# Gate and up products of two token blocks made 256 columns at a time

## The chip, the cores and the metric

The kernel runs on one core of a Trainium2 chip, in one launch. The core has a matrix engine (PE, with its weight loads shown apart as PEld), a vector engine (DVE), a scalar engine (ACT), a general engine (POOL) and a queue engine (SP) that issues most of the transfers. On-chip data lie in 128 partitions; matrix products land in PSUM, in tiles of 128 by 512 floats here. The metric is the device time of the whole launch in microseconds; lower is better.

## The reference

The reference is one transformer-like layer for 2048 tokens of width 640: a modulation vector, a layer norm, a long convolution (a state space kernel applied by FFT), a second layer norm, and a gated feed-forward part of width 1728. The change touches only the feed-forward part:

```python
def _B_ref(x, w1, w3, w2):
    gate = jnp.einsum("bsd,df->bsf", x, w1)
    up = jnp.einsum("bsd,df->bsf", x, w3)
    h = _silu(gate) * up
    out = jnp.einsum("bsf,fd->bsd", h, w2)
    return out
...
x = x + ga * _A_ref(h, ...)
h = _layernorm(x, axis=-1) * (1 + cb) + sb
x = x + gb * _B_ref(h, B_w1, B_w3, B_w2)
```

Everything is float32.

## The kernel before

The first 390 us or so make the convolution. The rest is the feed-forward part, in `ffn` (L755). It runs over four token blocks `b` of 512 tokens, and in each over 14 tiles of 128 hidden columns (`ORDER`: tile 0, then tile 13, which is half as wide, then 1 to 12).

To keep float32 accuracy at the rate of the type float32r, each operand is split into a high and a low part (`split`, L665): `x` into `xh` and `xl`, `w1` and `w3` into `wh` and `wl`, the hidden values into `ah` and `al`, `w2` into `w2h` and `w2l`. A product is three terms: high by high, high by low, low by high.

For each tile three steps follow each other in the program:

- `up` (L792) makes the gate and the up product, each in a PSUM tile `gu` of 128 hidden columns by 512 tokens: for each of the five 128-wide slices `k` of the width it makes the three terms `wh·xh`, `wh·xl`, `wl·xh` (L800 to L802), 15 matmuls that add into one tile. Each matmul has weights of 128 by 128 and a moving operand of 128 by 512. Tile 13 holds gate and up in one `gu`. A block so has 27 `gu` tiles and 405 such matmuls.
- `gate` (L805) makes the hidden values from the two tiles: a tanh on ACT (L813), two DVE operations (L814, L815), the split into `ah` and `al` (L666, L667). For tile 13 it is a longer chain over 64 partitions (L819 to L826).
- `down` (L829) multiplies the hidden values of the tile before by `w2` into the five accumulators `acc0` to `acc4` of the block: 15 matmuls a tile, 10 for tile 13.

The weights of each tile are loaded by SP (L713, L718) and split by ACT and DVE (L732, L733, L741, L745) ahead of their use. After the eighth tile of a block, `ln2` (L669) norms and transposes the next block's tokens into `xh` and `xl`; after a block's last tile `output` (L839) adds the result and stores it.

The `gu` tiles have three PSUM banks in turn, `wr`, `wh`, `wl`, `ah`, `al` two buffers each. Within these limits and the data's own order a scheduler of the build sets the order of the instructions on each engine; the engines then run their lists in order and wait for each other by semaphores.

Of the kernel before, what the change touches and what calls it, by code (L numbers as in the profile page):

```python
# [21 lines left out]
KT = D // P  # L22
# [260 lines left out]
class K:  # L283
# [508 lines left out]
    def up(self, b, tiles, xh, xl, ps):  # L792

        nc = self.nc
        gu = [[ps.tile([P, 512], F32, name=f"gu{b}_{m}{i}", tag="gu", bufs=3) for i in range(2 if m < 13 else 1)] for m, _, _ in tiles]
        every = [(pg, wh[:, i], wl[:, i]) for (m, wh, wl), g in zip(tiles, gu) for i, pg in enumerate(g)]
        for ks in [(k,) for k in range(KT)] if len(tiles) > 1 else [range(KT)]:
            for pg, wh, wl in every:
                for k in ks:
                    nc.tensor.matmul(pg, wh[:, k, :], xh[:, k, :], start=(k == 0), stop=False)  # L800
                    nc.tensor.matmul(pg, wh[:, k, :], xl[:, k, :], start=False, stop=False)  # L801
                    nc.tensor.matmul(pg, wl[:, k, :], xh[:, k, :], start=False, stop=(k == KT - 1))  # L802
        return gu

    def gate(self, b, m, gu, pool):  # L805
# [764 lines left out]
```

## Time and profile before

| | |
|---|---|
| time, median of 2 runs | 985.68 us (984.6 to 986.76) |
| the profiled execution's own time | 987.09 us |
| its span, first to last instruction | 985.3 us |
| PE / PEld busy, share of the span | 90% / 72% |
| DVE / ACT / POOL busy, share of the span | 68% / 50% / 29% |
| granted TensorE clock, mean | 0.972 |
| first matmul of the second block's `gu` | 553.79 us into the span |
| first matmul of the third block's `gu` | 694.82 us |
| first matmul of the fourth block's `gu` | 835.85 us |

The profile gives for each instruction its engine, source line, tiles and shape, its start and its length. The length of a matmul is modelled and reaches into the next one, since matmuls are pipelined: how fast a row of matmuls runs is read from their starts, not from their lengths. The start of one to the start of the next is called the step here. The float32r operands of matmuls are shown as f32 in the rows.

### The profile page before, as it was taken

To read this page: it belongs to the slowest core of one execution; us is meant where nothing else is said; L and a number is where in the kernel's file an instruction comes from. 1 tells how busy PE (TensorE), PEld (TensorE's weight loads), DVE (VectorE), ACT (ScalarE), POOL (GpSimd) and SP (SyncE) were. 2 spreads that over 40 slices of the span, in tenths; PEclk is the share of its full clock that TensorE was granted. 3 is DMA by queue.
4 is the path that set the end of the run, shared out by engine and by line. 5 is a ranking of instruction groups with operands and counts; after the bars stand their busy time and mean duration, and the time that the engine had idled before them with its cause. 6 is when DMAs were issued, how large, how long until landed. Compare 5 with 4: busy or idle time off the path is not lost.

```text
span 985.3 us, 20196 instructions
## 1 busy us (share of the span) xinstructions
PE 884.0 (90%) x8095; PEld 707.7 (72%) x8095; DVE 665.6 (68%) x1235; ACT 496.6 (50%) x829; POOL 287.9 (29%) x293
## 2 busy tenths in 40 slices
PE   1465787889999997999999999999999999999997
PEld 1133665767888873677788888888888888888885
DVE  6998999999999774677664464464644554754443
ACT  6878788879888741532243343342333333433321
POOL 0798799889899330100000000000000000000000
PEclk9885999999999999999999999999999999999999
DMA  9955453714131297997232354223353323543311
GB/s 207 271 173 200 115 140 89 176 46 118 36 94 45 62 271 217 223 234 181 58 111 76 107 150 118 80 85 103 100 154 93 108 80 93 141 120 88 104 31 53
DMA packets 141189, 122.03 MB, mean 124 GB/s; under 512 B 13480, under 2 KB 124840, under 8 KB 139688
## 3 DMA queue, kind: packets, MB, share of 16 engines
q1 hardware_dynamic: 140360, 119.84, 45.3%
q8 instruction: 63, 1.03, 0.5%
q10 hardware_dynamic: 736, 0.92, 0.3%
q14 instruction: 30, 0.25, 0.1%
HBM read 99.75 MB, written 20.97 MB: 123 GB/s over the span
## 4 chain that ended last, share of the span: by engine, by line
PE 70%; DVE 15%; ACT 4%; DMA 3%; issue 3%; SPq 2%; POOL 2%; DVEq 0%; ACTq 0%; POOLq 0%
PE acc L837 19%; PE gu L800 12%; PE gu L801 12%; PE gu L802 12%; DVE yy L157 3%; PE ps L157 3%; PE kps L157 2%; SPq L157 2%; DVE fp L157 2%; PE fz L157 2%; DVE hn L157 2%; DVE xx L157 2%; PE fk L157 2%; PE fh L157 2%; PE iy L652 1%
## 5 line engine op out<-in xcount | busy, mean ns | idle before, releaser
L800 PE MATMUL gu<-xh,wh 128*128 128x512 f32 x540 | 210.8, 392 | 0.1
L802 PE MATMUL gu<-xh,wl 128*128 128x512 f32 x540 | 210.3, 390 | 0.0
L801 PE MATMUL gu<-xl,wh 128*128 128x512 f32 x540 | 210.3, 390 | 0.0
L732 ACT ACTIVATE wh<-wr 128x640 fp32r<-128x640 f32 x105 | 71.9, 731 | 134.3 <-PE gu L801 131.0
L744 POOL MEMSET w2l<- 64x640 f32 x3 | 1.9, 630 | 444.6 <-PE acc L837 444.6
L800 PEld LDWEIGHTS gu<-xh,wh 128*128 128x128 f32 x540 | 101.7, 189 | 21.3 <-ACT xh L666 0.5
L802 PEld LDWEIGHTS gu<-xh,wl 128*128 128x128 f32 x540 | 101.4, 188 | 21.2
L801 PEld LDWEIGHTS gu<-xl,wh 128*128 128x128 f32 x540 | 101.6, 188 | 20.8
L813 ACT ACTIVATE th<-gu 128x512 f32<-128x512 f32 x52 | 31.1, 597 | 128.7 <-PE gu L802 128.5
L815 DVE TENSOR_TENSOR a<-a,gu 128x512 f32<-128x512 f32 x52 | 35.8, 688 | 85.6 <-PE gu L802 85.4
L157 POOL TENSOR_TENSOR yy<-e,e 128x512 f32<-128x512 f32 x80 | 86.2, 1093 | 16.5 <-PE kps L157 10.5
L814 DVE SCALAR_TENSOR_TENSOR a<-th,gu 128x512 f32<-128x512 f32 x52 | 35.7, 686 | 75.2 <-ACT th L813 75.1
L837 PE MATMUL acc<-w2h,ah 128*128 128x512 f32 x219 | 85.4, 390 | 0.0
L837 PE MATMUL acc<-w2l,ah 128*128 128x512 f32 x219 | 85.4, 390 | 0.0
L733 ACT ACTIVATE w2h<-w2r 128x640 fp32r<-128x640 f32 x54 | 39.9, 739 | 88.7 <-issue 52.2
L741 DVE TENSOR_TENSOR wl<-wr,wh 128x640 fp32r<-128x640 f32 x105 | 82.4, 819 | 0.0
L157 POOL TENSOR_TENSOR ph<-p,p 128x1024 int32<-128x1024 int32 x40 | 79.9, 1996 | 7.7 <-ACT tr L157 7.0
L745 DVE TENSOR_TENSOR w2l<-w2r,w2h 128x640 fp32r<-128x640 f32 (+1 forms) x54 | 44.4, 822 | 52.9 <-ACT w2h L733 52.7
L157 DVE TENSOR_TENSOR yy<-yy,tr 128x512 f32<-128x512 f32 (+1 forms) x80 | 75.5, 945 | 0.9 <-ACT tr L157 0.6
L837 PE MATMUL acc<-w2h,al 128*128 128x512 f32 x203 | 76.1, 390 | 0.0
L157 PE MATMUL kps<-yy,xx 128*32 128x64 f32 x2560 | 52.1, 237 | 24.7 <-DVE xx L157 21.6
L157 PEld LDWEIGHTS kps<-yy,xx 128*32 128x32 f32 x2560 | 45.6, 118 | 34.3 <-issue 17.2
(231 smaller groups left out, 1692.9 us busy)
## 6 DMA issues: line engine op xcount, KB each, us to landing
wr<-in_w SPq DMA_DIRECT2D x104, 320.0 KB, 3.6
w2r<-in_w SPq DMA_DIRECT2D x52, 320.0 KB, 3.0
zd<-zt SPq DMA_DIRECT2D x39, 256.0 KB, 2.8
iz<-zd SPq DMA_DIRECT2D x24, 320.0 KB, 7.0
xs<-in_x SPq DMA_DIRECT2D x16, 320.0 KB, 11.7
hs<-hb SPq DMA_DIRECT2D x20, 256.0 KB, 2.4
xb<-hs SPq DMA_DIRECT2D x20, 256.0 KB, 4.9
x<-in_x SPq DMA_DIRECT2D x16, 320.0 KB, 9.6
```

What stands on the lines that cost most here:

```text
L157: self.prev = self.k.order(f(*a, **kw), self.prev)
L732: self.nc.scalar.activation(wh[:, i], raw[:, i], AF.Copy)
L733: self.nc.scalar.activation(w2h, w2r, AF.Copy)
L741: eng.tensor_tensor(wl[:, i], raw[:, i], wh[:, i].bitcast(F32), op=ALU.subtract)
L745: eng.tensor_tensor(w2l[q], w2r[q], w2h[q].bitcast(F32), op=ALU.subtract)
L800: nc.tensor.matmul(pg, wh[:, k, :], xh[:, k, :], start=(k == 0), stop=False)
L801: nc.tensor.matmul(pg, wh[:, k, :], xl[:, k, :], start=False, stop=False)
L802: nc.tensor.matmul(pg, wl[:, k, :], xh[:, k, :], start=False, stop=(k == KT - 1))
L813: nc.scalar.activation(th, gu[0], AF.Tanh, scale=0.5)
L814: nc.vector.scalar_tensor_tensor(a, th, 1.0, gu[0], op0=ALU.add, op1=ALU.mult)
L815: nc.vector.tensor_mul(a, a, gu[1])
L837: nc.tensor.matmul(acc[k], *two(a, w), start=(m == 0 and i == 0), stop=(m == 12 and i == 2))
```

## The change

The gate and up products of blocks 1 and 2 (the second and the third) are made with a moving operand of 128 by 256 in place of 128 by 512, so with two matmuls for each one before. The sum in each `gu` tile is made of the same terms. Block 1 takes each term for both halves in turn, so that two matmuls with the same weights follow each other; block 2 takes the three terms of a slice for the first half and then the three for the second. Blocks 0 and 3 keep 512 columns; their matmuls are only issued from another line. Only the first matmul on a `gu` tile has the start flag, also where the second half is written for the first time.

```diff
             for pg, wh, wl in every:
+                halves = [slice(0, 256), slice(256, 512)]
                 for k in ks:
-                    nc.tensor.matmul(pg, wh[:, k, :], xh[:, k, :], start=(k == 0), stop=False)
-                    nc.tensor.matmul(pg, wh[:, k, :], xl[:, k, :], start=False, stop=False)
-                    nc.tensor.matmul(pg, wl[:, k, :], xh[:, k, :], start=False, stop=(k == KT - 1))
+                    terms = list(enumerate(((wh, xh), (wh, xl), (wl, xh))))
+                    pairs = [(t, c) for t in terms for c in halves] if b == 1 else [(t, c) for c in halves for t in terms] if b == 2 else [(t, slice(0, 512)) for t in terms]
+                    for (i, (w, x)), c in pairs:
+                        nc.tensor.matmul(pg[:, c], w[:, k, :], x[:, k, c], start=(k == 0 and i == 0 and c.start == 0), stop=(k == KT - 1 and i == 2),
+                                         skip_group_check=b in (1, 2))
```

PE's list shows it. In these rows `gu1_30` is the gate tile of block 1, tile 3, `gu2_30` that of block 2; `xh1`, `wh1_3` and so on are the operands; the shape is that of the output, and `x2` at a row's end stands for two like instructions. First the start of `gu1_30` on PE before:

```order
L800 MATMUL gu1_30_6827<-xh1_6109,wh1_3_6817 128x512
L801 MATMUL gu1_30_6827<-xl1_6110,wh1_3_6817 128x512
L802 MATMUL gu1_30_6827<-xh1_6109,wl1_3_6822 128x512
L800 MATMUL gu1_30_6827<-xh1_6109,wh1_3_6817 128x512
L801 MATMUL gu1_30_6827<-xl1_6110,wh1_3_6817 128x512
L802 MATMUL gu1_30_6827<-xh1_6109,wl1_3_6822 128x512
```

These are two slices of the width. The same place on PE now:

```order
L804 MATMUL gu1_30_6932<-xh1_6109,wh1_3_6922 128x256 x2
L804 MATMUL gu1_30_6932<-xl1_6110,wh1_3_6922 128x256 x2
L804 MATMUL gu1_30_6932<-xh1_6109,wl1_3_6927 128x256 x2
L804 MATMUL gu1_30_6932<-xh1_6109,wh1_3_6922 128x256 x2
L804 MATMUL gu1_30_6932<-xl1_6110,wh1_3_6922 128x256 x2
L804 MATMUL gu1_30_6932<-xh1_6109,wl1_3_6927 128x256 x2
```

Each matmul has become two of half the width that follow each other with the same weights. In block 2, one slice of `gu2_30` on PE now:

```order
L804 MATMUL gu2_30_8437<-xh2_7471,wh2_3_8427 128x256
L804 MATMUL gu2_30_8437<-xl2_7472,wh2_3_8427 128x256
L804 MATMUL gu2_30_8437<-xh2_7471,wl2_3_8432 128x256
L804 MATMUL gu2_30_8437<-xh2_7471,wh2_3_8427 128x256
L804 MATMUL gu2_30_8437<-xl2_7472,wh2_3_8427 128x256
L804 MATMUL gu2_30_8437<-xh2_7471,wl2_3_8432 128x256
```

Here the three terms go round once for the first half and once for the second.

The scheduler also moves the down product of tile 13 (`acc1x` from `ah1_13`) at the start of both blocks. Before, it stood on PE inside `gu1_20`, the gate tile of tile 2, behind seven of its 15 matmuls:

```order
L801 MATMUL gu1_20_6756<-xl1_6110,wh1_2_6746 128x512
L802 MATMUL gu1_20_6756<-xh1_6109,wl1_2_6751 128x512
L800 MATMUL gu1_20_6756<-xh1_6109,wh1_2_6746 128x512
L837 MATMUL acc14_6608<-ah1_13_6666,w2h1_13_6625 128x512
L837 MATMUL acc14_6608<-ah1_13_6666,w2l1_13_6629 128x512
L837 MATMUL acc10_6604<-w2h1_13_6625,ah1_13_6666 128x512
```

Now it stands on PE behind the last of `gu1_11`, ahead of `gu1_20`:

```order
L804 MATMUL gu1_11_6736<-xh1_6109,wh1_1_6725 128x256 x2
L804 MATMUL gu1_11_6736<-xl1_6110,wh1_1_6725 128x256 x2
L804 MATMUL gu1_11_6736<-xh1_6109,wl1_1_6730 128x256 x2
L840 MATMUL acc14_6638<-ah1_13_6711,w2h1_13_6655 128x512
L840 MATMUL acc14_6638<-ah1_13_6711,w2l1_13_6659 128x512
L840 MATMUL acc10_6634<-w2h1_13_6655,ah1_13_6711 128x512
```

All ten matmuls of that down product so come seven old `gu` matmuls sooner. In the step before it, the down product of tile 0 is taken accumulator by accumulator, three terms each, where two terms of three accumulators came first; and its second part stands behind eleven of the half-width matmuls of `gu1_10` where it stood behind eleven of full width. On DVE, ACT, POOL and SP the lists keep their order but for a few neighbours that change places around tile 13.

## The prediction

> **What bounds the kernel now.** I read the page first, its busy shares and its chain of waits: who ends last, and by which lines.
>
> ```profile
> PE 884.0 (90%) x8095; PEld 707.7 (72%) x8095; DVE 665.6 (68%) x1235; ACT 496.6 (50%) x829; POOL 287.9 (29%) x293
> ...
> PE 70%; DVE 15%; ACT 4%; DMA 3%; issue 3%; SPq 2%; POOL 2%; DVEq 0%; ACTq 0%; POOLq 0%
> PE acc L837 19%; PE gu L800 12%; PE gu L801 12%; PE gu L802 12%; DVE yy L157 3%; PE ps L157 3%; PE kps L157 2%; SPq L157 2%; DVE fp L157 2%; PE fz L157 2%; DVE hn L157 2%; DVE xx L157 2%; PE fk L157 2%; PE fh L157 2%; PE iy L652 1%
> ```
>
> The three lines that the change rewrites hold 36% of the chain, all as work of PE. Each matmul has a weight load of its own (8095 of both), also where two in a row take the same weights. Next the busy times in the stretch of blocks 1 and 2 (columns: stretch, length, busy time and count of PE, PEld, DVE, ACT, POOL, granted clock, DMA share, GB/s), then those of the `gu` tiles alone in each block (without POOL):
>
> ```profile
> 553.80:835.80 282.00, 282.00 (x1269) 234.06 (x1268) 144.83 (x208) 100.61 (x156) 1.26 (x2) 1.00 0.38 105
> ...
> 554.00:694.00 140.00, 94.10 (x405) 75.54 (x403) 18.58 (x27) 8.82 (x15) 1.00 0.38 105
> 695.00:835.00 140.00, 94.13 (x405) 75.53 (x404) 18.57 (x27) 8.84 (x15) 1.00 0.38 105
> ```
>
> PE is busy through all 282 us at the full clock, DVE about half and ACT a third of it. What is added to PE here moves the end by as much. The two blocks have 2 × 405 = 810 of the matmuls that are cut in two. The rate they run at stands in the chain in order of time (start, length, engine, line, count):
>
> ```profile
> 628.12 3.40 PE acc L837 x15
> 638.31 3.40 PE acc L837 x15
> 641.72 1.31 PE tp L691 x12
> ```
>
> These 15 have the shape of the `gu` matmuls: 3.40 / 15 = 226.7 ns a step, while the page's length for one is 390. The reader sees that the length says nothing here, the steps do. The timeline shows a weight load beside the matmul ahead of it:
>
> ```profile
> 640.19 0.39 PE L837 MATMUL acc<-w2h,ah 128*128 128x512 f32 x1
> 640.19 0.19 PEld L837 LDWEIGHTS acc<-w2l,ah 128*128 128x128 f32 x1
> 640.42 0.39 PE L837 MATMUL acc<-w2l,ah 128*128 128x512 f32 x1
> 640.42 0.19 PEld L837 LDWEIGHTS acc<-w2h,al 128*128 128x128 f32 x1
> ```
>
> The load for the next matmul starts as this one starts and ends within its step.
>
> **The matmuls themselves: 810 become 1620.** No float32r matmul of 256 columns is in the trace. The question is what share of the 226.7 ns is paid per column and what per matmul. Plain f32 matmuls with the same 128 by 128 weights give two widths, 512 in the row below and 128 in the `tp` row above:
>
> ```profile
> 379.44 3.60 PE L157 MATMUL awake<-wd,ident 128*128 128x512 f32 x8
> ...
> L157 PE MATMUL awake<-wd,ident x22: 592/593/697, 375.9 to 389.9; 128*128 128x512 f32 x22
> ```
>
> Eight lie in 3.60 us, the last with its own 0.593: (3.60 − 0.593) / 7 = 429.6 ns a step at 512 columns. `tp` gives 1.31 / 12 = 109.2 at 128. The slope is (429.6 − 109.2) / 384 = 0.834 ns a column, and 109.2 − 128 × 0.834 = 2.4 ns are left per matmul. A float32r column must cost less than f32's, since 226.7 is little over half of 429.6; if it is just half, 0.417, then 512 columns take 213.5 ns and 13.2 ns are left per matmul. This is an estimate, since it rests on the half. By it 256 columns take 106.8 + 13.2 = 120.0 ns, two of them 240.0, and each old matmul costs 13.3 ns more: 810 × 13.3 = 10.8 us.
>
> The bounds. Below: if the 226.7 were all per column, two halves would take as long as one whole, and the term is 0. A gain is excluded, since each half needs a load and a matmul for no fewer columns. Above there are two rows. The first is the step where PE comes back from transposes (timeline, start of block 1's second `gu`):
>
> ```profile
> 564.66 0.40 PE L801 MATMUL gu<-xl,wh 128*128 128x512 f32 x1
> 564.90 0.40 PE L802 MATMUL gu<-xh,wl 128*128 128x512 f32 x1
> 565.13 0.40 PE L800 MATMUL gu<-xh,wh 128*128 128x512 f32 x1
> ```
>
> Here the step is 0.47 / 2 = 235 ns for the same shape: the part per matmul is not constant but can be 235 − 213.5 = 21.5. With that, a half takes 128.3 and the term is 810 × (256.6 − 226.7) = 24.2 us. The second is how fast weight loads can follow each other; a row of loads with four-column matmuls shows nothing but them:
>
> ```profile
> 103.25 0.97 PEld L157 LDWEIGHTS pv<-ident,mc 128*128 128x128 f32 x8 [0.17 <-ACT mc L157]
> ```
>
> (0.97 − 0.19) / 7 = 111 ns from load to load. A load has 227 ns of cover before and 120 after: still hidden, with 9 ns to spare. I take 120.0, since 226.7 holds for all long rows of both blocks and 235 only for a few matmuls behind transposes.
>
> On a load's overlap the trace has the rows above, load and matmul with one start; the step of 226.7 is far under 111 + 213.5 = 324.5. The Trainium skill speaks against the change here: TensorE: Matmul & The Clock Gate, Part 3, section "The mechanism", says that weight loads overlap running matmuls only where their row groups differ. All loads here take all 128 rows. The trace disagrees at 512 columns, and the same page's Part 2, step ①, has a way out: a load into the background buffer may go ahead. What the rule would give is the third rival below.
>
> **The order of halves and terms.** Block 1 puts the same weights in two matmuls in a row, block 2 three different terms on one half. Since loads are not dropped for equal weights before, I cost both orders alike: 405 × 13.3 = 5.4 us each. The waiting ACT and DVE operations follow the last matmul of a tile, which is the last half of the last term in both. More instructions must be fetched; the page's row for them is small, and PE can issue far faster than a pair of load and matmul in 120 ns:
>
> ```profile
> q8 instruction: 63, 1.03, 0.5%
> ...
> 342.21 1.10 PE kps L157 x60
> ```
>
> Sixty small pairs went in 1.10 us, 18 ns a pair. Both at nothing.
>
> **The moved down products.** Tile 13's comes seven `gu` matmuls sooner. It waits for the last step of the longer gate chain:
>
> ```profile
> 567.88 0.39 PE L837 MATMUL acc<-ah,w2h 128*128 128x512 f32 x1
> ...
> 574.28 0.69 DVE L826 TENSOR_TENSOR ah<-a,th 64x512 fp32r<-64x512 f32 x1 [1.69 <-ACT th L825]
> ```
>
> `ah` is ready at 574.97. From tile 0's down product at 567.88 PE now has nine matmuls of 512, eleven of 256, six of 512, nineteen and thirty of 256 ahead of the moved one: 15 × 0.227 + 60 × 0.120 = 10.6 us, so it comes at 578.5, with 3.5 us to spare. Behind it on PE stands `gu1_20`, which would wait too. For tile 0, the low part `al` is now third in place of seventh:
>
> ```profile
> 564.07 0.68 DVE L667 TENSOR_TENSOR al<-a,ah 128x512 fp32r<-128x512 f32 x1
> ```
>
> It is ready at 564.75 and asked for at 568.3. Both moves cost nothing. DVE, ACT and SP get some 5 us more for each block's same work, and nothing of it ends a wait of PE now.
>
> **The sum.** 10.8 us on PE, all of it on the path. Against the profiled execution (span 985.3, its time 987.09, so 1.8 around the span) that gives 997.9; its time is 1.4 over the median of 985.68, and against that median 985.68 + 10.8 = **996.5 us**, 1.1% slower. A measurement of this kernel can tell some 2%, 19.7 us, from no change.
>
> **The rivals.**
>
> *The cost follows the columns.* If float32r is simply slower per column than half of f32 (0.443 against 0.417), halves cost half. For it: PE reads its operand faster there, which may not run at the full rate. Against it: 235 and 226.7 at one width show that something other than columns moves the step. With the 2.4 ns per matmul of plain f32 the time is 985.68 + 810 × 2.4 / 1000 = 987.6; without, 985.7. The same skill page's section "Back-to-back issue gap" has such a rule, columns at 2.4 GHz and 2.5 ns per matmul, which would give 2.0 us here (an estimate from its figures); its 215.8 ns at 512 columns falls short of the 226.7 measured.
>
> *The loads set the pace; slower from a point on.* In `gu` of both blocks the load fills 111 of 120 ns. If the 13.2 ns lie behind the load rather than beside it, a half takes 111 + 13.2 = 124.2 and the time is 985.68 + 810 × 21.7 / 1000 = 1003.3; if the step takes the 235 ns form, 128.3 and 1009.9. The bound of 2% is passed when a half takes over (226.7 + 24.3) / 2 = 125.5 ns. For it: the cover shrinks from 116 ns to 9, and the 235 ns rows come right behind transposes, which run at the loads' pace. Against it: loads are as long (0.19) under matmuls as alone.
>
> *The loads are not hidden at all.* With 111 + 106.8 = 217.8 per half the time is 985.68 + 810 × 208.9 / 1000 = 1155. The overlap shown above speaks against it.
>
> *A wait in the place of the moved products* would have to use up 3.5 us at each of two places first; it could add a few us.
>
> **How the numbers follow.** The forecast (halves at about 120): 0.55. Cost by columns: 0.13. Loads set the pace: 0.25, of which 0.15 over 125.5 ns. Not hidden: 0.04. The rest, a wait or something that no row shows: 0.03, slower. So slower by over 2%: 0.15 + 0.04 + 0.03 = 0.22. Within 2%: 0.55 + 0.13 + 0.10 = 0.78 less 0.01 for faster, which no row offers: 0.77. The range goes from 987.0 (columns, with little per matmul) to 1009.0 (near the 235 ns form); outside lie the last two cases and the edges of the first two rivals, together under 0.2.
>
> **What would show it.** The blocks begin so far with these matmuls:
>
> ```profile
> 553.79 0.39 PE L800 MATMUL gu<-xh,wh 128*128 128x512 f32 x1
> ...
> 694.82 0.39 PE L800 MATMUL gu<-xh,wh 128*128 128x512 f32 x1
> ...
> 835.85 0.39 PE L800 MATMUL gu<-xh,wh 128*128 128x512 f32 x1
> ```
>
> Blocks 1 and 2 take 141.03 us each. In the profile of the changed kernel PE still busy through both blocks, 1620 matmuls of 128x256 with 1620 loads, blocks 1 and 2 each 5.4 us longer, a step of 120 ns in long rows, blocks 0 and 3 as before. A step of 113 speaks for the columns, over 124 for the loads, over 200 for no overlap. Blocks 1 and 2 of different length would show that the order of halves matters, which I cost at nothing. PE idle ahead of an `acc` at the start of a block would show a moved wait.

## The result and the profile after

| | before | after |
|---|---|---|
| time, median of 2 runs each | 985.68 us (984.6 to 986.76) | 996.97 us (995.57 to 998.37) |
| ratio, 95% interval | | 1.0098 (1.0072 to 1.0124) |
| span of the profiled execution | 985.3 us | 993.8 us |
| block 1, block 2, from first `gu` matmul to first `gu` matmul | 141.03, 141.03 us | 146.63, 146.64 us |

The kernel became 11.3 us, or 1.0%, slower: within the 2% that were called no difference that a measurement can tell, though the interval lies clear of 1.

The page of the changed kernel, its busy shares, its chain of waits, and the group of `gu` matmuls (out and operands, shape, count, busy time, mean length, which mixes the two widths here):

```profile
PE 893.4 (90%) x8905; PEld 748.9 (75%) x8905; DVE 666.3 (67%) x1235; ACT 496.5 (50%) x829; POOL 287.9 (29%) x293
...
PE 73%; DVE 12%; DMA 5%; ACT 4%; issue 3%; SPq 2%; POOL 1%; DVEq 0%; ACTq 0%; POOLq 0%
PE gu L804 38%; PE acc L840 19%; PE ps L157 4%; DVE yy L157 3%; DMA xs<-in_x 3%; PE fz L157 2%; PE kps L157 2%; PE fk L157 2%; PE fh L157 2%; DVE fp L157 2%; DVE xx L157 2%; DVE hn L157 1%; PE iy L652 1%; SPq L157 1%; ACT tr L157 1%
L804 PE MATMUL gu<-xh,wh 128*128 128x256 f32 (+1 forms) x810 | 235.8, 320 | 0.7 <-ACT xh L666 0.7
```

PE has 810 matmuls and 810 loads more (8905 for 8095), the other engines as many instructions and as much busy time as before. The chain in order of time shows where the time went. First the first `gu` matmuls of block 0, the beginning of block 1 and a tile in it, then block 2 from its first `gu` matmuls to the down product of tile 13, then the start of block 3:

```profile
394.38 9.19 PE gu L804 x39
...
551.22 7.19 PE gu L804 x60
558.41 3.43 PE acc L840 x15
...
631.90 7.19 PE gu L804 x60
639.09 3.43 PE acc L840 x15
...
697.85 7.19 PE gu L804 x60
705.05 3.43 PE acc L840 x15
708.91 3.58 PE gu L804 x30
712.50 2.07 PE acc L840 x9
714.57 1.43 PE gu L804 x12
716.00 1.39 PE acc L840 x6
717.38 5.75 PE gu L804 x48
723.14 2.29 PE acc L840 x10
...
844.49 6.80 PE gu L804 x30
```

60 matmuls of 256 columns take 7.19 us, 119.8 ns a step, where 30 of 512 take 6.80, 226.7. The down product behind halves takes 3.43 us for 3.40. A tile goes from 10.20 to 10.62 us. (The chain has block 1 at 551.22, where its first matmul starts at 551.06; the differences between blocks are the same.) The rows follow each other without a gap, at the places of the moved down products too: block 2 needs 27.58 us from 697.85 to the end of the tenth `acc` matmul of tile 13 (723.14 + 2.29 = 725.43). There are 150 half matmuls and 40 whole ones in that stretch and four transposes of some 0.11 us: 18.0 + 9.1 + 0.4 = 27.5. Nothing is left for a wait.

The busy times in the two blocks (stretch, length, busy time and count of PE, PEld, DVE, ACT, POOL, granted clock, DMA share, GB/s):

```profile
551.20:697.80 146.60, 146.60 (x1041) 138.12 (x1040) 72.22 (x104) 51.09 (x79) 0.63 (x1) 1.00 0.37 102
697.80:844.40 146.60, 146.60 (x1041) 138.11 (x1040) 73.53 (x104) 49.57 (x77) 0.63 (x1) 1.00 0.37 102
```

PE is still busy throughout at the full clock; the loads now fill 94% of the stretch in place of 83% (117 of 141 us), by their shown length of 0.19 us, which like a matmul's is more than the step at which they can follow each other (111 ns). The two blocks together are 11.2 us longer. From start to start the `gu` matmuls take 5.2 us more in each block and the down products 0.4 more. The span grew by only 8.5 since block 1 began 2.7 us sooner in this execution. Of these, 2.1 lie ahead of the first `gu` matmul (at 394.38 in place of 396.49 us), in the convolution, which the change does not touch, and 0.6 in block 0, whose matmuls are the same (156.7 us in place of 157.3).

### The profile page after: what moved, and what is told of

Read it like the earlier page. It is cut to its first block, busy times and chain, and to the rows that moved or that the text cites. A ratio compares the mean times of both kernels' runs of the same rounds, so it can differ in the third digit from the quotient of the medians.

```text
span 993.8 us, 21812 instructions
## 1 busy us (share of the span) xinstructions
PE 893.4 (90%) x8905; PEld 748.9 (75%) x8905; DVE 666.3 (67%) x1235; ACT 496.5 (50%) x829; POOL 287.9 (29%) x293
## 4 chain that ended last, share of the span: by engine, by line
PE 73%; DVE 12%; DMA 5%; ACT 4%; issue 3%; SPq 2%; POOL 1%; DVEq 0%; ACTq 0%; POOLq 0%
PE gu L804 38%; PE acc L840 19%; PE ps L157 4%; DVE yy L157 3%; DMA xs<-in_x 3%; PE fz L157 2%; PE kps L157 2%; PE fk L157 2%; PE fh L157 2%; DVE fp L157 2%; DVE xx L157 2%; DVE hn L157 1%; PE iy L652 1%; SPq L157 1%; ACT tr L157 1%
## 5 line engine op out<-in xcount | busy, mean ns | idle before, releaser
L804 PE MATMUL gu<-xh,wh 128*128 128x256 f32 (+1 forms) x810 | 235.8, 320 | 0.7 <-ACT xh L666 0.7
L804 PE MATMUL gu<-xh,wl 128*128 128x256 f32 (+1 forms) x810 | 236.4, 319 | 0.0
L804 PE MATMUL gu<-xl,wh 128*128 128x256 f32 (+1 forms) x810 | 236.3, 319 | 0.0
L804 PEld LDWEIGHTS gu<-xh,wh 128*128 128x128 f32 x810 | 145.3, 191 | 12.6 <-ACT xh L666 1.0
L804 PEld LDWEIGHTS gu<-xl,wh 128*128 128x128 f32 x810 | 144.7, 191 | 11.1 <-DVE xl L667 0.2
L804 PEld LDWEIGHTS gu<-xh,wl 128*128 128x128 f32 x810 | 144.8, 191 | 10.6
## 6 DMA issues: line engine op xcount, KB each, us to landing
xs<-in_x SPq DMA_DIRECT2D x16, 320.0 KB, 11.2
```

The source lines that it names most:

```text
L804: nc.tensor.matmul(pg[:, c], w[:, k, :], x[:, k, c], start=(k == 0 and i == 0 and c.start == 0), stop=(k == KT - 1 and i == 2), skip_group ...
```

## The experiments

The theory that the prediction stood on: a float32r matmul costs 0.417 ns a column and some 13 ns beside, its weight load runs beside the matmul ahead of it and takes 111 ns, and what lasts longer sets the step. The step of 120 alone rules out a cost that follows the columns only (113 ns). It does not rule out that loads set the 120: that a load takes 120 ns while a stream runs at the full rate.

**Steps of many shapes.** Put into block 2 of the kernel before, behind the gate and up products of the sixth tile:

```diff
+                    if (b, i) == (2, 5):
+                        self.probe(wh, ps)
...
+    def probe(self, wh, ps):
+
+        nc = self.nc
+        pt = ps.tile([P, 512], F32, name="probe", tag="gu", bufs=3)
+        flat = wh.rearrange("p a k f -> p (a k f)")
+        for cols, n in ((128, 512), (128, 384), (128, 320), (128, 256), (128, 224), (128, 192), (128, 128), (128, 64),
+                        (64, 512), (64, 256), (64, 128), (32, 512), (32, 256), (32, 128)):
+            for i in range(24):
+                nc.tensor.matmul(pt[:cols, :n], flat[:, 512:512 + cols], flat[:, :n], start=True, stop=True)
+        f = flat.bitcast(F32)
+        for n in (512, 256, 128):
+            for i in range(6):
+                nc.tensor.matmul(pt[:, :n], f[:, 512:640], f[:, :n], start=True, stop=True)
```

> The kernel before with a row of extra matmuls put into block 2 behind the gate and up products of the sixth tile; their result is read by nobody. 24 float32r matmuls of each shape, then six plain f32 calls of three widths. Read: the step from start to start of each shape. Theory (0.417 ns a column and 13.2 ns per matmul, loads of 128 columns every 111 ns beside it): 128 weight columns give 226.7 ns at 512 moving columns, 173 at 384, 147 at 320, 120 at 256, then 111 flat at 224, 192, 128 and 64. Rival, loads set the 120: 120 flat from 256 down to 64. Rival, cost by columns (0.443): 170 at 384, 142 at 320, 113 at 256. On whose the 13.2 ns are: if they go with the load's columns, 64 weight columns give about 220 at 512 and 113 at 256, and 32 give 217 and 110; if they go with the matmul whatever its weights, 227 and 120 for both. Plain f32: about 430 per instruction at 512, 216 at 256, 111 at 128. Time: about 50 to 60 us over before.

The groups by shape (rows by columns of the weights, shape of the moving operand, count, busy time, mean length). In a row of n the step is the busy time less one length, over n − 1:

```profile
L815 PE MATMUL probe<-wh 128*128 128x512 f32 x24 | 5.6, 389 | 0.0
...
L815 PE MATMUL probe<-wh 128*128 128x384 f32 x24 | 4.3, 335 | 0.0
L815 PE MATMUL probe<-wh 128*128 128x320 f32 x24 | 3.7, 309 | 0.0
L815 PE MATMUL probe<-wh 128*128 128x256 f32 x24 | 3.0, 283 | 0.0
L815 PE MATMUL probe<-wh 128*64 128x256 f32 x24 | 2.9, 277 | 0.0
L815 PE MATMUL probe<-wh 128*32 128x256 f32 x24 | 2.9, 276 | 0.0
L815 PE MATMUL probe<-wh 128*128 128x224 f32 x24 | 2.8, 274 | 0.0
L815 PE MATMUL probe<-wh 128*128 128x192 f32 x24 | 2.8, 273 | 0.0
L815 PE MATMUL probe<-wh 128*128 128x128 f32 x24 | 2.8, 273 | 0.0
L815 PE MATMUL probe<-wh 128*128 128x64 f32 x24 | 2.8, 275 | 0.0
...
L815 PE MATMUL probe<-wh 128*32 128x128 f32 x24 | 1.6, 223 | 0.0
L815 PE MATMUL probe<-wh 128*64 128x128 f32 x24 | 1.6, 222 | 0.0
```

The busy time is rounded to 0.1 us, so these steps are good to 2 ns: 227 at 512, 172 at 384, 147 at 320, 118 at 256, and 110 at 224, 192, 128 and 64 alike. From start to start of single matmuls the usual steps are 227, 173, 147, 120 and 109 to 115. The three wider rows lie on one line, 0.417 ns a column and 13.3 beside, and this line gives 120.0 at 256: no load is needed to explain it. So 128 columns of float32r weights cost 111 ns however little is streamed, and above some 235 moving columns (where 0.417 a column and 13 make 111) the stream and its 13 ns set the step. The rival of 120 flat falls: at 224 columns the step is below 120. The rival by columns falls too: it had 170, 142 and 113. At 256 columns the load is hidden by 9 ns, as the prediction had it.

With 64 or 32 columns of weights neither expectation held as a whole. At 256 columns the step is 113 to 114 with both, 7 ns beside the columns: 113 was to come with 64 if the 13 ns went with the load's columns, but 32 were to give 110. At 128 columns it is 60 with both, again 7 beside the columns. At 512 columns the steps of both go up and down between 224 and 236, some 230 in the mean (apart from the stretch in the last section), where 220 and 217, or 227 for both, were expected. So the extra is smaller with a narrow load at 256 and 128 columns, but not at 512, and it does not go with the load's columns.

The plain f32 calls run as two matmuls each (12 for six calls):

```profile
L819 PE MATMUL probe<-wh 128*128 128x512 f32 x12 | 5.4, 596 | 0.0
...
L819 PE MATMUL probe<-wh 128*128 128x256 f32 x12 | 2.8, 379 | 0.0
```

They gave what was expected: from start to start 429 ns at 512 columns and 216 at 256, some 2.5 ns beside 0.834 a column, and 111 to 112 at 128, where the load decides.

The kernel took 1041.37 us in a single run, 53.8 over the 987.6 of the kernel before on that chip.

**One block alone.** In the changed kernel, the halves of the other block are taken out:

```diff
-                    pairs = [(t, c) for t in terms for c in halves] if b == 1 else [(t, c) for c in halves for t in terms] if b == 2 else [(t, slice(0, 512)) for t in terms]
+                    pairs = [(t, c) for t in terms for c in halves] if b == 1 else [(t, c) for c in halves for t in terms] if b == 9 else [(t, slice(0, 512)) for t in terms]
...
-                                         skip_group_check=b in (1, 2))
+                                         skip_group_check=b == 1)
```

In the second kernel `b == 9` stands in place of `b == 1` instead, and the last line has `b == 2`.

> Halves in block 1 alone (each term for both halves in turn). Theory: 405 x 13.3 ns and a little at the edges, block 1 at 146.6 us in place of 141.0, +5.6 us, ratio about 1.006. Rival, the moved down products or the order matter: another length of block 1 than in the changed kernel, or of a block that was left alone.

> Halves in block 2 alone (the three terms for the first half, then for the second). Theory: the same +5.6 us, ratio about 1.006, block 2 at 146.6 us. Rival, equal weights in a row are cheaper or dearer: another price than block 1 alone.

Block 1 alone: 991.66 us against 987.6 of before (18 runs on that chip), ratio 1.005 (1.0032 to 1.0067). Block 2 alone: 993.16, ratio 1.006 (1.004 to 1.0079). The medians moved by 4.1 and 5.6 us, where 5.6 was expected of both; the intervals overlap, and the lengths of the blocks are the sharper measure. The chain shows the same starts of tiles; of the kernel with halves in block 1 the start of block 1, of block 2 and of block 3:

```profile
551.62 7.19 PE gu L804 x60
...
698.25 6.80 PE gu L804 x30
...
839.28 6.80 PE gu L804 x30
```

of the kernel with halves in block 2 the same three:

```profile
552.90 6.80 PE gu L804 x30
...
693.92 7.19 PE gu L804 x60
...
840.56 6.80 PE gu L804 x30
```

146.63 and 141.03 us in the first, 141.02 and 146.64 in the second. Each block pays 5.6 us for itself and nothing in the other, and both orders of halves and terms cost the same: equal weights in two matmuls in a row save nothing, and three terms on one half lose nothing.

**All four blocks.**

```diff
-                    pairs = [(t, c) for t in terms for c in halves] if b == 1 else [(t, c) for c in halves for t in terms] if b == 2 else [(t, slice(0, 512)) for t in terms]
+                    pairs = [(t, c) for t in terms for c in halves] if b in (0, 1) else [(t, c) for c in halves for t in terms] if b in (2, 3) else [(t, slice(0, 512)) for t in terms]
...
-                                         skip_group_check=b in (1, 2))
+                                         skip_group_check=True)
```

> Halves in all four blocks, 1620 matmuls cut in two. Theory: four times 5.6, +22 us, time about 1008, ratio about 1.023; a little less in block 0 where PE waits in places. Rival, the price shrinks or grows with PE's load (clock, fetches): not four times.

1010.45 us against 987.6, ratio 1.0233 (1.0189 to 1.0277): +22.9 us, four times 5.7. In its trace blocks 1 and 2 take 146.63 us each again, and block 0 takes 162.1 in place of 157.3. The price is additive. The median passes 2%, but the interval reaches below it, so that these runs do not settle whether the change does.

**More weight columns, types, and what ran before.** The same place, other shapes:

```diff
...
+        for cols, n in ((96, 512), (96, 256), (96, 128), (128, 512), (128, 128), (128, 512)):
+            for i in range(24):
+                nc.tensor.matmul(pt[:cols, :n], flat[:, 512:512 + cols], flat[:, :n], start=True, stop=True)
+        f = flat.bitcast(mybir.dt.bfloat16)
+        for n in (512, 256, 128):
+            for i in range(24):
+                nc.tensor.matmul(pt[:, :n], f[:, 512:640], f[:, :n], start=True, stop=True)
```

> Again extra matmuls in block 2, 24 of each: float32r with 96 weight columns at 512, 256 and 128 moving columns; with 128 weight columns at 512, 128 and 512 again; then the same bytes read as bfloat16, 128 weight columns at 512, 256 and 128. Theory A, the 13 ns belong to float32r's stream running beside a load of more than 64 columns: 96 columns give 120 at 256 (113.5 was measured with 64 and 32, 120 with 128), bfloat16 gives 216 and 109, some 11 ns less a matmul than float32r. Theory B, they belong to any matmul with a full load at this rate: bfloat16 gives 227 and 120 too. The second row of 512 behind the row of 128: 227 throughout if what ran before does not matter, some 235 at first if the 235 ns behind transposes come from a row that runs at the loads' pace. At 128 columns 96 weight columns give 83 to 85 if a load's time goes with its columns.

The groups by shape again:

```profile
L814 PE MATMUL probe<-wh 128*128 128x512 f32 x48 | 11.4, 393 | 0.0
L814 PE MATMUL probe<-wh 128*96 128x512 f32 x24 | 5.7, 392 | 0.0
L818 PE MATMUL probe<-wh 128*128 128x512 bf16 x23 | 5.1, 379 | 0.1
L814 PE MATMUL probe<-wh 128*96 128x256 f32 x24 | 3.0, 278 | 0.0
...
L818 PE MATMUL probe<-wh 128*128 128x256 bf16 x24 | 2.8, 272 | 0.0
L814 PE MATMUL probe<-wh 128*96 128x128 f32 x24 | 2.2, 246 | 0.0
L818 PE MATMUL probe<-wh 128*128 128x128 bf16 x24 | 1.5, 219 | 0.0
```

And of the loads of 128 columns, float32r and bfloat16:

```profile
L814 PEld LDWEIGHTS probe<-wh 128*128 128x128 f32 x72 | 11.6, 189 | 1.9
...
L818 PEld LDWEIGHTS <-wh 128*128 128x128 bf16 x72 | 6.0, 98 | 3.4 <-issue 0.3
```

Bfloat16, with loads of as many columns, takes (5.1 − 0.379) / 22 = 215 ns at 512, 110 at 256 and 56 at 128: 2.5 ns beside the columns, as plain f32 has. So theory B falls, and of theory A the main part holds: the 11 ns more go with float32r. Whether with its stream or with its load is not shown, since a bfloat16 load is shorter as well (shown length 98 ns against 189; with 56 from matmul to matmul it can take no more than that). With bfloat16 the same cut would cost some 3 ns a matmul in place of 13. The other part of theory A did not come: 96 columns of weights give some 116 at 256, alternating from 112 to 121 (expected 120), so at 256 the extra grows with the load from 64 columns on and does not jump behind 64; at 512 they give 230. At 128 columns 96 columns of weights give 85, where the load sets the step: its time goes with its columns (85 for 96, 111 for 128).

The 48 float32r matmuls of 512 lie in two rows of 24, one behind 96 columns of weights and one behind 128 columns, each with 128 moving columns and at the loads' pace: (11.4 − 2 × 0.393) / 46 = 230.7 ns in the mean, where the row in the first of these kernels had 226.7. In the list of starts the second row begins 292, 235, 233, 236, 224, 231, 236, 228, 233, 231 and then keeps to 226 and 227; the first begins 280, 230, 231, 236, 228, 233, 231. The 235 ns form that the prediction took for a bound thus comes from what ran before, as expected, and is left after seven to ten matmuls. It does not need the loads' pace, though: in the changed kernel the down products behind halves, which run at 120, begin 233, 236, 229, 232, 231 as well. Behind 512 columns they had begun at 228.

**Quarters.**

```diff
-halves = [slice(0, 256), slice(256, 512)]
+halves = [slice(o, o + 128) for o in range(0, 512, 128)]
```

> Four matmuls of 128 columns for each old one in blocks 1 and 2. Theory: the load (111 to 112 ns) sets the step, 4 x 111.5 = 446 in place of 226.7, 810 x 219 ns = +178 us, about 1165; if the array's clock is halved in part of it, since it streams less than half the time, more. Rival, only the price per matmul counts and loads are hidden: 4 x 66.5 = 266, +32 us, about 1019.

1168.27 us against 987.52, ratio 1.1816 (1.1753 to 1.1879): +180.8 us, against +178 by the theory and +32 by its rival. Two tiles of block 1 in the chain:

```profile
614.69 13.35 PE gu L804 x120
628.04 3.51 PE acc L840 x15
631.55 13.35 PE gu L804 x120
```

13.35 / 120 = 111.3 ns: the load sets the step, and twice the cut costs not twice but sixteen times as much. The granted clock stayed at 1.00 through both blocks, which the expectation left open. The down product behind the quarters takes 3.51 us: the 235 ns form at its beginning.

**Unequal halves.**

```diff
-halves = [slice(0, 256), slice(256, 512)]
+halves = [slice(0, 384), slice(384, 512)]
```

> 384 and 128 columns in place of 256 and 256, in blocks 1 and 2. If only one load can be ahead of the running matmul: 173.3 + 111 = 284.5, +58 ns on 810, +47 us, about 1034. If loads can run further ahead, so that the wide matmul covers both: 173.3 + 66.7 = 240, as with equal halves, +11 us, about 998.

1036.78 us against 987.52, ratio 1.0486 (1.0432 to 1.054): +49.3 us. The chain in block 1 and in block 2 (a tile each):

```profile
621.24 8.54 PE gu L804 x60
...
763.03 8.57 PE gu L804 x60
```

8.54 / 30 = 284.7 ns for a pair, 285.7 in block 2, as with one load ahead (284.5) and not as with more (240). The loads show it too: in block 1 they start 108 and 178 ns apart in turn. Under a wide matmul the load of the narrow one starts early, but the load after it waits until the narrow one starts. A load that the wide matmul would have covered is not made earlier than one matmul ahead. (From start to start the matmuls here show 58 and 228 in turn. Where the width changes, a matmul's shown start can lie ahead of the shown end of its load, so the pair is read.)

## Why the prediction was right

**The forecast's step was the measured one.** 120.0 ns a half was forecast and 119.8 measured; +10.8 us was forecast and +11.3 measured between the medians, 11.2 between the block lengths. The term itself came to 10.4 us, from start to start of the `gu` matmuls, mostly since a half that follows a down product starts its row with 113 or 114 ns. The other 0.8 is the start of each down product behind halves, 3.43 for 3.40 us, which the sum had not: the 235 ns form, which the prediction knew from behind transposes and held for a bound on the halves.

**The part per matmul.** The estimate took a float32r column for half a plain f32 column. No row of the trace showed this; the forecast hung on it, and it came true. The row of shapes bears it out: 0.417 ns and 13.3 hold at 256, 320, 384 and 512 columns. The slope of plain f32 rested on transposes at 128 columns (109.2), close to the 111 of the loads, where a load could have set the step; 0.834 and 2.4 give 215.9 at 256, and 216 was measured. The 13.3 are no rest of a wrong slope, and bfloat16's 2.5 show that they go with float32r.

**The loads' cover.** It was put at 111 of 120 ns, and the cut at 224 columns and in quarters shows the point from which loads decide. The rival in which loads set the pace was right in its mechanism, which begins 20 columns or so below what the change did, and wrong in its price: the 13 ns lie beside the load, not behind it. No overlap at all would have given over 200 ns a step, and 119.8 were measured. The Trainium skill's rule that loads overlap running matmuls only where row groups differ (TensorE: Matmul & The Clock Gate, Part 3, "The mechanism") does not hold for these loads, which take all 128 rows; by the unequal halves one load runs ahead, and only one.

**The moved down products and the order of terms** cost no wait, as forecast: PE has no gap at these places, and blocks 1 and 2 are of one length, whether cut together or alone. The new order was not undone by itself, so this rests on the absence of a wait, not on a run without the move. The spare time was less than the 3.5 us of the prediction: in block 1 the last part of `ah` is done at 573.08 + 0.69 = 573.77 us (DVE, L829), and PE asks for it at 576.34, 2.6 us later.

**What was noise.** The median moved by 11.3, the spans by 8.5. The difference is the 2.7 us by which block 1 began sooner, 2.1 of them in the first 396 us, and was not part of any term.

## What to carry to other kernels

Read a row of matmuls by its steps, and split a step into a part per column, a part per matmul, and the weight load beside it: halving a width costs only the part per matmul as long as half the stream still covers the load, and from there on what the load takes beyond the stream (here 13 ns a matmul down to some 235 columns, then 111 ns less the stream's: 31 at 192, 58 at 128, 84 at 64). Where PE has no idle time, such a cut can be priced even if the new width is not in the trace: here to 4% (10.8 for 11.2 us), from two widths of another type and one assumption on how the types compare. Pairing equal weights or placing a narrow matmul behind a wide one did not help.

## What the runs showed of the hardware that was not expected

A row behind narrow matmuls fell into a stretch of half the clock. In the first kernel of shapes the 24 matmuls of 512 columns with 64 weight columns took far longer than those with 32:

```profile
L815 PE MATMUL probe<-wh 128*64 128x512 f32 x24 | 7.3, 472 | 0.0
L815 PE MATMUL probe<-wh 128*32 128x512 f32 x24 | 5.7, 394 | 0.0
```

The windows of that kernel show the granted clock (behind the busy times of the five engines) in the 3.41 us ahead of the slow ones, with them, and behind them:

```profile
769.46:772.87 3.41, 3.41 (x32) 3.38 (x32) 0.00 (x0) 0.00 (x0) 0.00 (x0) 1.00 0.00 0
772.87:776.28 3.41, 3.41 (x9) 1.78 (x8) 0.00 (x0) 0.00 (x0) 0.00 (x0) 0.50 0.00 0
776.28:779.69 3.41, 3.41 (x16) 2.00 (x15) 0.00 (x0) 0.00 (x0) 0.00 (x0) 1.00 0.00 0
```

Seven steps of 427 ns, twice 213.5, lie in it, right behind some 10 us of full loads with 224 to 64 moving columns; the last 2.7 us of these streamed 64 columns, by 0.417 ns a column 27 of 111 ns. Narrow weights alone do not bring it: the row with 32 columns of weights kept the full clock. The Trainium skill (TensorE: Matmul & The Clock Gate, Part 1, "What's actually happening") has a gate that halves PE's clock after an idle window of about 3.4 us. The length agrees, 3.41 us at 0.50; but PE was not idle here by the profile, it only streamed little. The quarters ran two blocks at the loads' pace, streaming 53 of 111 ns, with down products between, and kept the full clock. What decides between the two was not tried.

What float32r pays beside its columns is no constant of the machine. It is 13.3 ns with 128 columns of weights in a settled row, 20 or so in the first matmuls behind narrower ones, some 7 with 64 or 32 columns of weights at 256 and 128 moving columns, and with 32 columns at 512 again (5.7 − 0.394) / 23 − 213.5 = 17 ns. That it comes from the load's reads meeting a stream of four bytes a column at the full rate would fit bfloat16 and plain f32 paying 2.5, but this is argued and not shown; what sets the 7 and the 17 stays open.
